# Selective attention into a hard-swish MLP: mask by selection from the fifth pair, one normalization for two heads over two banks, and moved queue work

## The chip, the cores and the metric

The kernel runs on one core of one Trainium2 chip. The metric is the device time of one execution in microseconds (us). TensorE (PE) does the matrix products, VectorE (DVE) and ScalarE (ACT) the elementwise work, GpSimd (POOL) casts, selects and issues DMAs, SyncE (SP) only issues DMAs.

## The reference

There are 8 batches of 8 heads with 576 positions and 64 channels. The attention has a decay that comes from `s`, and its output goes through a two-layer MLP.

```python
scores = scale * np.matmul(q, k.transpose(0, 1, 3, 2))        # scale = 1/8
causal = np.triu(np.ones((S, S), dtype=bool), k=1)
cum = np.cumsum(np.maximum(s, 0.0), axis=-1)
bias = -(cum[:, :, :, None] - cum[:, :, None, :])
scores = np.where(causal, -1e9, scores + np.minimum(bias, 0.0))
attn = np.exp(scores - np.max(scores, axis=-1, keepdims=True))
attn = attn / (np.sum(attn, axis=-1, keepdims=True) + 1e-09)
x = np.matmul(attn, v)      # then heads side by side: [4608, 512]
h = x @ w_in                # [512, 2048]
g = h * np.clip(h + 3.0, 0.0, 6.0) / 6.0
out = g @ w_out             # [2048, 512]
```

## The kernel before

**Attention.** The 64 heads go in 32 pairs; pair `p` holds heads 2p and 2p+1 (called head 0 and head 1 of the pair, `hh` in the code), and pairs are numbered from 0. Scores are computed transposed, keys on partitions, queries in columns. Queries and keys of a pair lie in `qks[p % 4]`, channels in rows 0 to 63, and in rows 64 to 67 the running sums of `s`, so that the decay comes out of the same product. Per head there are three score groups of 512 columns: `scores(p, hh, 0)` holds the four diagonal blocks of 128 keys, groups 1 and 2 what lies beside them. `corner(p)` does the last 64 positions of both heads. ACT takes the exponential of each into `P` (three buffers) or `PC`.

**The causal mask.** In pairs 0 to 7 (`NPROD` = 8) the diagonal group begins with one product of 512 columns that adds a large negative number above the diagonal (L377), and the corner with one of 128 columns (L441). In pairs 8 to 31 there is no such product: rows 68 to 127 of `qks` hold a stair of 60 steps that makes the excluded scores small, and after the exponential GpSimd sets them to zero with an affine select (`shut_out`, L426). The stair is copied into `qks` by GpSimd (in the iterations of pairs 5 to 7) and ACT (8 and 9) with `set_stair`.

**The order of queries.** A pair's queries and keys are loaded as tokens (`load_qk`), transposed on PE (`transpose_in`, L266 and L253) into PSUM and copied into `qks` by DVE and ACT (`transpose_out`, L310, L298, L332). In pairs 3 to 6 the queries stand in another, "mixed" order, for which these copies have runs of 16 elements (L298). The rows of running sums must then be in that order too (`load_aug`; the mixed copy of the rows is made at L840), and x is put back by the matrix `perm`.

**Values and normalization.** `av(p, hh, 0)` and `av(p, hh, 1)` multiply P with the values into a tile O of five blocks of 65 columns, the 65th being the sum of weights. `norm(p, hh)` on DVE is a reciprocal of the five sums (L503) and a product (L504) into `x`. In pairs 0 to 6, 11 and 31 `transpose_x` turns x into `xT` over PE and DVE (L518, L523), in the others `crossbar_x` does it with a DMA.

**The MLP.** It goes in blocks of 512 rows. A group `m1` is four products of 512 columns with `w_in` (L547) into `ph`; ACT makes `tr` of it (L562), DVE `gT` (L563). A group `m2` is four products with `w_out` (L574); four of them fill one `po` of 128 rows, which DVE scales and SP stores (L590, L593). `m2` takes two 128-row blocks in turn: its even steps go to one, its odd steps to the other.

**The order.** The schedule is written by hand. `group()` puts the next `m1` or `m2` where the loop over pairs calls it, by a written plan for the first blocks and then in turn. Pair 4 is the first with MLP groups; before it only attention runs. In each pair `av(p, 0, ...)` and `norm(p, 0)` stand in its own iteration, `av(p, 1, ...)` and `norm(p, 1)` in the next one. A pair from 5 on ends so:

```python
av(p, 0, 1)
norm(p, 0)
group()
```

Engines run their instructions in the order of the program, and a semaphore holds each until its inputs are ready and its output is free.

**PSUM.** There are eight banks: two for `ph`, two for `s` (scores; while `early` is set, the `ph` banks take scores too), two for `po`, one for `o`, one for `t`. O lies in `o`, or for head 1 in `po` (pairs 0 to 6) and `t` (from pair 9); transposed inputs and x lie in `t`, and before the first `m2` also in `po` (`t_bank`).

**The queues.** GpSimd issues tokens, weights (`load_w_in`, `load_w_out`) and most rows of running sums; SP issues v, the first rows, the crossbar transpositions and the outputs. `pool_mid` and `pool_end` hold GpSimd's work of a pair: select, cast of v, select. In pairs 4 to 7 `pool_mid` stood ahead of the pair's first scores in the program, without selects.

Of the kernel before, what the change touches and what calls it, by code (L numbers as in the profile page):

```python
# [18 lines left out]
def kernel(  # L19
# [31 lines left out]
    VW = 66  # L51
    NROW = 1
    NWARM = (11, 2, 6)
    HALVES = (slice(0, 288), slice(288, SEQ))
# [3 lines left out]

    grp = (np.arange(128) * 61 // 128)[None, :]
    steps_r = np.arange(1, 61)[:, None]  # L60
    stair = np.zeros((128, 2, 128), np.float32)
    stair[68:, 0] = np.where(grp < steps_r, 1.0, 0.0)
    stair[68:, 1] = np.where(grp == steps_r, NEG_BIG, 0.0)
    stair_dram = nc.inline_tensor(stair.astype(np.float16), name="stair")

# [28 lines left out]
    ident2 = keep("ident2", [128, 128], F16)  # L94
    stair_sb = keep("stair_sb", [128, 2, 128], F16)
    bias3 = keep("bias3", [128, 1], F32)
# [62 lines left out]
    def load_aug(p, eng):  # L159
        for hh in range(2):  # L160
# [6 lines left out]
            )  # L167

    def load_w_in(c):
        nc.gpsimd.dma_start(  # L170
            out=w_in_sb[:, :, 512 * c : 512 * (c + 1)],
            in_=moe_w_in[:, 512 * c : 512 * (c + 1)].rearrange(
                "(kc p) f -> p kc f", p=128
            ),
        )
# [34 lines left out]
    early = [True]  # L210
    turn = [0]

    def s_bank(shape, name):
# [4 lines left out]
    def t_bank(other, name):  # L218
        if not done[2] and other:
            return psum.tile([128, 640], F16, tag="po", bufs=2, name=name)  # L220
        return psum.tile([128, 640], F16, tag="t", name=name)
# [51 lines left out]
    def mixed(p, i):  # L273
        return i == 0 and PPB - 1 <= p < NPROD - 1

# [93 lines left out]
    def scores(p, hh, g):  # L369
        qT, kT = qk_of(p, hh)  # L370
        pt = Pof(p, hh)
        S = s_bank([128, 512], "S")
        by_product = p < NPROD
        if g == 0:
            rows = slice(0, 68 if by_product else 128)
            if by_product:
# [46 lines left out]

    def shut_out(ap, w):
        part = ap.rearrange("p (t c) -> p t c", c=w)
        nc.gpsimd.affine_select(  # L426
            out=part,
            in_=part,
            pattern=[[0, part.shape[1]], [1, w]],
            compare_op=ALU.is_ge,  # L430
            fill=0.0,
            base=0,
            channel_multiplier=-1,
        )

    def corner(p):
        S = s_bank([128, 2, 64], "Sc")
        by_product = p < NPROD
        rows = slice(0, 68 if by_product else 128)
        if by_product:  # L440
# [29 lines left out]
    def av(p, hh, part):  # L470
        va, pt = vas[p % NVA], Pof(p, hh)
        if part == 0:

            tag = "o" if not hh or NPROD - 1 <= p < NPE - 2 else "po" if p < NPROD else "t"
            O[p, hh] = psum.tile(
                [128, 5, 65], F32, tag=tag, bufs=2 if tag == "po" else 1, name="O"
            )
        o = O[p, hh]
# [11 lines left out]
        else:  # L490
# [5 lines left out]
            block(4, 4, PCs[p % 2][:, c : c + 128], start=False, stop=True)  # L496

    def norm(p, hh):
        o = O.pop((p, hh))
        if hh == 0:  # L500
# [12 lines left out]
    def transpose_x(p):  # L513
        b, hp = p // PPB, p % PPB
        x = X.pop(p)
        pt = t_bank(True, "ptx")
        for t in range(5):
# [49 lines left out]
    def m2(n, i):  # L567
        t4, fq = 2 * (i // 8) + i % 2, i % 8 // 2
        if fq == 0:
            po = psum.tile([128, 512], F32, tag="po", bufs=2, name="po")  # L570
            pos[n, t4] = po
# [120 lines left out]

    def set_stair(i, copy, heads=(0, 1)):
        for hh in heads:
            copy(
                out=qks[i][64:128, hh, :, 64 * hh : 64 * hh + 640].rearrange(
                    "p i (t c) -> p i t c", c=128
                ),
                in_=stair_sb[64:128, :, None, :].to_broadcast([64, 2, 5, 128]),
            )  # L700

    fill(nc.vector, xT[:, 0, 0:SEQ], 0.0)

    def warm(n):
        W = psum.tile([128, 512], F32, tag="o", name="W")
        for _ in range(n):
            nc.tensor.matmul(
                W, lhsT=xT[:, 0, 0:128], rhs=xT[:, 0, 0:512], start=True, stop=True
            )
# [119 lines left out]
    warm(NWARM[2])  # L829
    load_aug(1, nc.gpsimd)  # L830
    load_v(1, nc.sync)
    load_aug(2, nc.sync)
    cast_v(0)
    for i in range(2):
        load_qk(3, i)
    load_v(2, nc.sync)
    cast_v(1)
    for i in range(2):
        load_qk(4, i)
    nc.gpsimd.tensor_copy(  # L840
        out=mix(rows_of[0][0:32, 0, 0:SEQ]), in_=unmix(C["c"][0:32])
    )

# [3 lines left out]
    for p in range(NP):  # L847
# [27 lines left out]
        def pool_mid():  # L875
            if p >= NPROD:
                shut_out(Pof(p, 0)[:, 0:512], 128)
            if nxt:
                cast_v(p + 1)
            if p in (5, 6, 7):  # L880
                set_stair((p + 3) % NQK, nc.gpsimd.tensor_copy)
            if p == 13:
                new_rest()
                cum4(1, nc.gpsimd, whole)
                cum5(1, nc.gpsimd.tensor_copy, whole)

        def pool_end():
            if p >= NPROD:
                shut_out(PCs[p % 2][:, 0:128], 64)
                shut_out(Pof(p, 1)[:, 0:512], 128)  # L890
            if p >= NPROD and p != 9 and p + 2 < NP:
                if p == 14:
                    cum6(1, nc.gpsimd, whole)
                load_aug(p + 2, nc.gpsimd)

        if p >= PPB:
            for fn, c in {
                4: ((I, 2),),
                5: ((I, 3),),
                6: ((U, 0), (U, 1), (U, 2), (U, 3)),  # L900
                7: ((U, 4), (U, 5), (U, 6), (U, 7)),
            }.get(p, ()):
                fn(c)
        if PPB <= p < NPROD:
            pool_mid()
            if p == 4:
                load_aug(7, nc.gpsimd)
            elif p in (6, 7):
                load_aug(p + 2, nc.gpsimd)
# [6 lines left out]
        if p == 2:  # L916
            nc.sync.dma_start(out=stair_sb, in_=stair_dram.ap())
        if p == 10:
# [12 lines left out]
        if p < PPB:  # L931
            scores(p, 0, 0)
            scores(p, 0, 1)
            get(0)
            scores(p, 0, 2)
            corner(p)
            if p:
                av(p - 1, 1, 0)
                av(p - 1, 1, 1)
                norm(p - 1, 1)  # L940
            get(1)
            scores(p, 1, 0)
            scores(p, 1, 1)
            av(p, 0, 0)
            scores(p, 1, 2)
            if p:
                transpose_x(p - 1)
            av(p, 0, 1)
            norm(p, 0)
            continue  # L950

        if p == PPB:
            early[0] = False
            scores(p, 0, 0)
            av(p - 1, 1, 0)
            av(p - 1, 1, 1)
# [11 lines left out]
        else:  # L968
            scores(p, 0, 0)
            if p >= NPROD:  # L970
                pool_mid()
            get(0)
            group()
            scores(p, 0, 1)
# [10 lines left out]
        corner(p)  # L985
        if p in (8, 9):
            set_stair(3, nc.scalar.copy, (p - 8,))
        elif p == 11:
            new_sum()
# [7 lines left out]
        scores(p, 1, 0)  # L997
        if p >= NPROD:
            pool_end()
        if PPB < p < NPE - 1:  # L1000
# [64 lines left out]
```

## Time and profile before

| | |
|---|---|
| runs | 354.62, 355.29 and 932.81 us, median 355.29 |
| profiled execution | 354.79 us, span 353.1 us, TensorE clock 1.00 |
| PE busy | 345.1 us, 2926 matmuls |
| DVE, ACT, POOL busy | 230.2, 224.7, 169.7 us |
| second MLP matrix, L574 | 145.9 us in 576 products, 379 ns each |
| first MLP matrix, L547 | 148.1 us in 576 products, 379 ns each |
| O, L481 | 47.9 us in 896 products, 193 ns each |
| exponentials, L422 | 111.3 us in 192 |
| normalization, L503 and L504 | 64 each, 186 and 492 ns |
| select, L426, 512 columns | 48, 651 ns |
| mask product, L377 and L441 | 16 and 8, 379 and 219 ns |
| stair copies, L695 | 6 on GpSimd, 2 on ACT, 1253 and 1255 ns |

The span is the time from the first to the last instruction that the profile shows. A line "L504 DVE TENSOR_TENSOR x<-O,rl 128x320" is line 504 of the program, its engine and operation, its output and inputs, and its shape. In a group's line there follow busy time, mean duration of one, and the idle time of the engine ahead of it with what ended it. In a timeline the columns are start and length in us; matmuls are pipelined, so that a length holds the pipeline too and what one costs is read from start to start.

### The profile page before, as it was taken

The page shows a single profiled execution, that of the slowest core. Times are in us where ns is not written, and L with a number is a line of the kernel's source. Part 1 is how long each engine was busy: PE and PEld are TensorE (multiplying, and loading weights), DVE is VectorE, ACT ScalarE, POOL GpSimd, SP SyncE. Part 2 cuts the span into 40 slices and gives each one's busy share as a digit, 9 for nine tenths or more (in the row PEclk, how much of TensorE's full clock was granted, in tenths as well). Part 3 has the DMA queues.
Part 4 walks back from the last instruction along what each step waited for, and adds up shares of the span by engine and source line. Part 5 has one row for each costly group of instructions (what it writes and reads, how often), then busy time and mean ns, then how long its engine had stood idle before and what let it go on. Part 6 is the DMA issues. An engine that isn't in the chain of part 4 may idle for free.

```text
span 353.1 us, 7778 instructions
## 1 busy us (share of the span) xinstructions
PE 345.1 (98%) x2926; PEld 191.0 (54%) x2926; DVE 230.2 (65%) x476; ACT 224.7 (64%) x397; POOL 169.7 (48%) x296
## 2 busy tenths in 40 slices
PE   8999999999999999999999999999999999999995
PEld 3775666555555555555555555555555444444442
DVE  7996997676868677666666666757654544544531
ACT  6987896787787667666776666666664334443310
POOL 8977799676778656455555555555310000000000
PEclk9999999999999999999999999999999999999999
DMA  9999999999999999998798959997120100101112
GB/s 164 152 208 209 199 185 182 117 181 196 154 136 100 190 219 188 173 211 186 168 167 198 179 144 197 181 180 164 38 75 14 59 29 34 59 2 59 59 50 72
DMA packets 144782, 48.35 MB, mean 137 GB/s; under 512 B 130648, under 2 KB 139784, under 8 KB 144744
## 3 DMA queue, kind: packets, MB, share of 16 engines
q1 hardware_dynamic: 117112, 37.54, 54.0%
q0 software_dynamic: 27392, 10.03, 24.8%
q8 instruction: 23, 0.38, 0.4%
q10 hardware_dynamic: 240, 0.28, 0.2%
q14 instruction: 15, 0.12, 0.1%
HBM read 37.36 MB, written 9.44 MB: 133 GB/s over the span
## 4 chain that ended last, share of the span: by engine, by line
PE 90%; DVE 4%; ACT 3%; issue 1%; DMA 1%; ACTq 0%
PE po L574 35%; PE ph L547 34%; PE O L481 7%; PE S L403 7%; PE S L388 4%; DVE qk L310 1%; PE pt L266 1%; ACT P L422 1%; DMA s_all<-in_s_dram 1%; DVE x L504 1%; PE ptx L518 1%; PE Sc L454 1%; ACT tr L562 1%; PE S L377 1%; DVE qk L332 1%
## 5 line engine op out<-in xcount | busy, mean ns | idle before, releaser
L563 DVE SCALAR_TENSOR_TENSOR gT<-tr,ph 128x512 f16<-128x512 f32 x144 | 98.9, 687 | 97.6 <-ACT tr L562 96.5
L547 PE MATMUL ph<-xT,w_in_sb 128*128 128x512 f16 x576 | 148.1, 379 | 0.0
L574 PE MATMUL po<-w_out_sb,gT 128*128 128x512 f16 x576 | 145.9, 379 | 0.0
L562 ACT ACTIVATE tr<-ph,bias 128x512 f32<-128x512 f32 x144 | 99.0, 688 | 73.0 <-PE ph L547 70.6
L422 ACT ACTIVATE P<-S 128x512 f16<-128x512 f32 x192 | 111.3, 595 | 37.5 <-PE S L388 22.3
L547 PEld LDWEIGHTS <-w_in_sb 128*128 128x128 f16 x576 | 51.4, 97 | 44.2
L574 PEld LDWEIGHTS <-gT 128*128 128x128 f16 x576 | 50.0, 97 | 46.5 <-issue 0.2
L426 POOL TENSOR_SCALAR_AFFINE_SELECT P<-P 128x512 f16<-128x512 f16 x48 | 31.3, 651 | 44.4 <-ACT P L422 44.4
L403 PE MATMUL S<-qk 68*128 68x448 f16 (+3 forms) x256 | 49.0, 272 | 0.5 <-ACT P L422 0.5
L481 PE MATMUL O<-va,P 128*128 128x65 f16 x896 | 47.9, 193 | 0.3 <-ACT P L422 0.3
L481 PEld LDWEIGHTS <-P 128*128 128x128 f16 x896 | 39.2, 97 | 14.0 <-ACT P L422 0.5
L230 DVE COPY qk<-jt 64x768 f16<-64x768 f16 x84 | 36.8, 439 | 1.2
L403 PEld LDWEIGHTS <-qk 68*128 68x128 f16 x256 | 23.7, 98 | 24.5 <-issue 0.9
L162 POOL DMA_DIRECT2D qk<-rows_of x56 | 32.8, 588 | 1.1 <-PE S L403 0.3
L504 DVE TENSOR_TENSOR x<-O,rl 128x320 f16<-128x320 f32 x64 | 31.5, 492 | 2.2
L590 DVE TENSOR_SCALAR ob<-po 128x512 f32<-128x512 f32 (+1 forms) x36 | 24.3, 676 | 8.3 <-PE po L574 7.6
L388 PEld LDWEIGHTS <-qk 128*128 128x128 f16 (+1 forms) x256 | 18.9, 97 | 14.0 <-DVE qk L310 1.7
L426 POOL TENSOR_SCALAR_AFFINE_SELECT PC<-PC 128x128 f16<-128x128 f16 x24 | 7.0, 293 | 39.9 <-ACT PC L462 39.8
L388 PE MATMUL S<-qk 128*128 128x128 f16 (+1 forms) x256 | 24.8, 219 | 1.0 <-DVE qk L332 0.5
L206 POOL CAST va<-vraw 128x512 f16<-128x512 f32 x32 | 21.0, 656 | 4.7 <-DMA vraw<-in_v_dram 2.4
L310 DVE COPY qk<-pt 64x576 f16<-64x576 f16 x22 | 17.6, 805 | 6.2 <-ACT qk L310 5.9
L202 POOL CAST tok<-raw 128x576 f16<-128x576 f32 x28 | 18.0, 679 | 0.0
(79 smaller groups left out, 201.9 us busy)
## 6 DMA issues: line engine op xcount, KB each, us to landing
out_dram<-ob SPq DMA_DIRECT2D x35, 256.0 KB, 2.0
vraw<-in_v_dram SPq DMA_DIRECT2D x64, 128.0 KB, 4.0
raw<-in_q_dram SPq DMA_DIRECT2D x14, 288.0 KB
raw<-in_k_dram SPq DMA_DIRECT2D x14, 288.0 KB
tok<-in_q_dram POOLq DMA_DIRECT2D x18, 144.0 KB, 5.2
tok<-in_k_dram POOLq DMA_DIRECT2D x18, 144.0 KB, 5.9
w_in_sb<-in_moe_w_in_dram POOLq DMA_DIRECT2D x4, 512.0 KB, 8.5
w_out_sb<-in_moe_w_out_dram POOLq DMA_DIRECT2D x8, 256.0 KB, 7.1
```

What stands on the lines that cost most here:

```text
L162: eng.dma_start(out=qks[p % NQK][64:68, hh, :, 64 * hh : 64 * hh + SEQ], in_=rows_of[g // 32].rearrange("(r g) i t -> g r i t", g=32)[g % ...
L230: copies[par](out=qk[0:64, :, i, 128 * par : 128 * par + 256 * n].rearrange("p h (s two c) -> p h s two c", two=2, c=128)[:, :, :, 0, :], ...
L388: mm(S[:, c], lhsT=kT[rows, c], rhs=qT[rows, c], start=(j == 0 and not by_product), stop=(j == 3 and p >= NROW),)
L403: mm(S[:, c : c + w], lhsT=kT[0:68, 128 * j : 128 * (j + 1)], rhs=qT[0:68, 128 * (j + 1) : SEQ], start=(c == 0), stop=(c != 0 and p >= NROW),)
L422: nc.scalar.activation(out=pt[:, c], in_=S, func=AF.Exp, scale=0.125)
L426: nc.gpsimd.affine_select(out=part, in_=part, pattern=[[0, part.shape[1]], [1, w]], compare_op=ALU.is_ge, fill=0.0, base=0, channel_multip ...
L481: mm(o[:, i, :], lhsT=lhsT, rhs=va[:, hh, j, 0:65], **kw)
L504: nc.vector.tensor_tensor(out=X[p][:, :, hh, :], in0=o[:, :, 0:64], in1=rl.to_broadcast([128, 5, 64]), op=ALU.mult,)
L547: mm(ph, lhsT=w_in_sb[:, kc, ft * 128 : (ft + 1) * 128], rhs=xT[:, kc, n * 512 : (n + 1) * 512], start=(kc == 0), stop=(kc == NKC - 1),)
L562: nc.scalar.activation(out=tr, in_=ph, func=AF.Relu, bias=bias3[:, 0:1])
L563: nc.vector.scalar_tensor_tensor(out=gTs[n][:, ft, :], in0=tr, scalar=6.0, in1=ph, op0=ALU.min, op1=ALU.mult)
L574: mm(po, lhsT=gTs[n][:, ft, t4 * 128 : (t4 + 1) * 128], rhs=w_out_sb[:, ft, :], start=(ft == 0), stop=(ft == NFT - 1),)
```

## The change

1. **Select from the fifth pair.** The mask products stay in pairs 0 to 3 alone (`NMASK` = 4). Pairs 4 to 7 take the stair and the select. The select gets a pattern for the mixed order.
2. **A shorter stair by DMA.** The stair has seven steps of 16 columns in rows 68 to 74, in two versions, for plain and mixed order, and is loaded straight into `qks` by SP (`load_stair`); the copies on GpSimd and ACT are gone.
3. **One normalization.** A tile `OO` of two banks replaces `o` and one bank of `po`. In pairs 0 to 2 and 4 to 6 head 0's O lies in half 0 and head 1's in half 1, and one reciprocal and one product serve both (`norm_pair`), in the place of head 1's. In pairs 0 to 2 `av(p, 0, ...)` moves into the next iteration. From pair 7 on half 0 takes O, and half 1 every second 128-row block of `m2`. The transposed x uses the bank `t`, except that of pair 3.
4. **Third pair's queries mixed.** `mixed` begins with pair 2.
5. **Queues.** `pool_mid` and `pool_end` hold the selects of pairs 4 to 7 and the weight loads, behind the first scores; rows of pairs 1, 7, 8 and 9 are issued by SP; the mixed copy of the rows comes before the second cast of v. In pairs 6 to 9 the next pair's queries are copied out around a group.

```diff
+    NMASK = PPB
+    NSTAIR = 7
...
+    grp = (np.arange(128) // 16)[None, :]
+    steps_r = np.arange(1, NSTAIR + 1)[:, None]
...
+    def load_stair(p, eng):
+        eng.dma_start(
+            out=qks[p % NQK][68 : 68 + NSTAIR], in_=stair_drams[mixed(p, 0)].ap()
+        )
...
+    OO = psum.tile([128, 2, 512], F32, tag="oo", name="OO")
+
+    def paired(p):
+        return p < PPB - 1 or PPB <= p < NPROD - 1
...
     def mixed(p, i):
-        return i == 0 and PPB - 1 <= p < NPROD - 1
+        return i == 0 and PPB - 2 <= p < NPROD - 1
...
-        by_product = p < NPROD
+        by_product = p < NMASK
         if g == 0:
-            rows = slice(0, 68 if by_product else 128)
+            rows = slice(0, 68 if by_product else 68 + NSTAIR)
...
-            tag = "o" if not hh or NPROD - 1 <= p < NPE - 2 else "po" if p < NPROD else "t"
-            O[p, hh] = psum.tile(
-                [128, 5, 65], F32, tag=tag, bufs=2 if tag == "po" else 1, name="O"
-            )
+            if hh and p >= NPE - 2:
+                O[p, hh] = psum.tile([128, 5, 65], F32, tag="t", name="O")
+            else:
+                half = hh if p < NPROD - 1 else 0
+                O[p, hh] = OO[:, half, 0:325].rearrange("p (i c) -> p i c", c=65)
...
+    def norm_pair(p):
+        o = OO[:, :, 0:325].rearrange("p h (i c) -> p h i c", c=65)
+        X[p] = work.tile([128, 5, 2, D], F16, tag="x", name="x")
+        rl = work.tile([128, 2, 5, 1], F32, tag="rl2", name="rl2")
+        nc.vector.reciprocal(out=rl, in_=o[:, :, :, 64:65])
+        nc.vector.tensor_tensor(
+            out=X[p].rearrange("p i h d -> p h i d"),
+            in0=o[:, :, :, 0:64],
+            in1=rl.to_broadcast([128, 2, 5, 64]),
+            op=ALU.mult,
+        )
+
     def norm(p, hh):
+        if paired(p):
+            if hh:
+                norm_pair(p)
+            return
...
-        pt = t_bank(True, "ptx")
+        pt = t_bank(p == PPB - 1, "ptx")
...
         if fq == 0:
-            po = psum.tile([128, 512], F32, tag="po", bufs=2, name="po")
+            if len(pos) % 2:
+                po = OO[:, 1]
+            else:
+                po = psum.tile([128, 512], F32, tag="po", name="po")
...
         def pool_mid():
-            if p >= NPROD:
-                shut_out(Pof(p, 0)[:, 0:512], 128)
+            shut_out(p, Pof(p, 0)[:, 0:512], 128)
             if nxt:
                 cast_v(p + 1)
-            if p in (5, 6, 7):
-                set_stair((p + 3) % NQK, nc.gpsimd.tensor_copy)
+            for fn, c in {
+                4: ((I, 2),),
+                5: ((I, 3), (U, 0), (U, 1)),
+                6: ((U, 2), (U, 3), (U, 4)),
+                7: ((U, 5), (U, 6), (U, 7)),
+            }.get(p, ()):
+                fn(c)
...
         if p == 2:
-            nc.sync.dma_start(out=stair_sb, in_=stair_dram.ap())
+            for i in range(PPB + 1, NPROD):
+                load_stair(i, nc.sync)
+        if p in (4, 6, 7):
+            n = 7 if p == 4 else p + 2
+            if p != 4:
+                load_stair(n, nc.sync)
+            load_aug(n, nc.sync)
+        elif p == 8:
+            load_stair(10, nc.sync)
...
             get(0)
+            if p:
+                av(p - 1, 0, 0)
+                av(p - 1, 0, 1)
             scores(p, 0, 2)
             corner(p)
+            get(1)
             if p:
                 av(p - 1, 1, 0)
                 av(p - 1, 1, 1)
                 norm(p - 1, 1)
-            get(1)
             scores(p, 1, 0)
             scores(p, 1, 1)
-            av(p, 0, 0)
             scores(p, 1, 2)
             if p:
                 transpose_x(p - 1)
-            av(p, 0, 1)
-            norm(p, 0)
+            if p == PPB - 1:
+                av(p, 0, 0)
+                av(p, 0, 1)
+                norm(p, 0)
             continue
```

## The prediction

> **What bounds the kernel now.** Pairs are numbered from 0, so the fifth pair is pair 4. I read the page first: busy time, then the chain that ended last.
>
> ```profile
> PE 345.1 (98%) x2926; PEld 191.0 (54%) x2926; DVE 230.2 (65%) x476; ACT 224.7 (64%) x397; POOL 169.7 (48%) x296
> ...
> PE 90%; DVE 4%; ACT 3%; issue 1%; DMA 1%; ACTq 0%
> ```
>
> The program is TensorE from end to end. An average over stages hides where that is so, so next the windows (columns: length, then busy us of PE, PEld, DVE, ACT, POOL):
>
> ```profile
> 9.90:26.20 16.30, 15.43 (x265) 12.31 (x263) 15.04 (x32) 14.98 (x32) 14.23 (x25) 1.00 1.13 184
> ...
> 33.00:61.00 28.00, 28.00 (x318) 17.94 (x317) 23.79 (x46) 23.16 (x45) 24.18 (x33) 1.00 1.18 191
> 120.00:265.00 145.00, 145.00 (x1273) 81.36 (x1271) 96.11 (x203) 99.41 (x177) 73.61 (x137) 1.00 0.86 166
> ```
>
> Pairs 0 to 3 (9.9 to 26.2) load PE, DVE and ACT alike. From 33 on PE never idles, so there a removed column is gained and a new wait is paid in full. The timeline shows what paces pairs 0 to 3, here the step from pair 2 to pair 3:
>
> ```profile
> 20.29 0.30 ACT L462 ACTIVATE PC<-Sc 128x128 f16<-128x128 f32 x1
> 20.44 0.81 ACT L310 COPY qk<-pt 64x576 f16<-64x576 f16 x1
> ...
> 21.29 0.81 DVE L310 COPY qk<-pt 64x576 f16<-64x576 f16 x1 [0.31 <-ACT qk L310]
> ...
> 22.15 0.23 PEld L388 LDWEIGHTS <-qk 68*128 68x128 f16 x4 [0.35 <-DVE qk L310]
> 22.16 0.40 PE L388 MATMUL S<-qk 68*128 68x128 f16 x4
> ```
>
> This is a ring: first scores of pair 2 at 18.34, its three exponentials, the corner's, ACT's half of pair 3's key copy, DVE's half, first scores of pair 3 at 22.16: 3.82 us a turn.
>
> Last, the end of a pair in the steady part, around the normalization of its first head:
>
> ```profile
> 156.04 1.03 PE L547 MATMUL ph<-xT,w_in_sb 128*128 128x512 f16 x4
> 156.91 0.44 PE L481 MATMUL O<-va,P 128*128 128x65 f16 x9
> 157.11 0.69 ACT L562 ACTIVATE tr<-ph,bias 128x512 f32<-128x512 f32 x1 [0.27 <-PE ph L547]
> 157.19 0.19 PE L481 MATMUL O<-va,PC 128*128 128x65 f16 x1
> 157.22 1.03 PE L574 MATMUL po<-w_out_sb,gT 128*128 128x512 f16 x4
> 157.83 0.69 DVE L563 SCALAR_TENSOR_TENSOR gT<-tr,ph 128x512 f16<-128x512 f32 x1 [1.64 <-ACT tr L562]
> 158.44 0.19 DVE L503 RECIPROCAL rl<-O 128x5 f32<-128x5 f32 x1
> 158.66 0.49 DVE L504 TENSOR_TENSOR x<-O,rl 128x320 f16<-128x320 f32 x1
> ```
>
> PE goes from the last product into O (157.19) to the second MLP matrix (157.22) in 0.03 us. DVE, in order, first does gT of the group before (it needs ACT, which needs PE's group of 156.04) and has normalized O only at 159.15. Nobody waits for that today.
>
> **What the Trainium skill says.** "TensorE: Matmul & The Clock Gate", step-by-step section: only weight loads are pulled ahead, matmuls stay in program order, so a matmul that waits holds all behind it. The trace agrees: PE's order above is the program's. "PSUM — Partial Sum Buffer", the section on bank collisions: guard by bank; its summary says to read one bank while a matmul writes a different one. The trace agrees: L574 at 157.22 fills one bank while L504 reads another. So the chip needs no wait between the halves of OO; whether there is one is the program's affair. "VectorE: DVE Perf Modes", why PSUM operands drop a tier: fp32 from PSUM runs at single rate; L504 takes 492 ns for 320 elements. "TensorE: Matmul & The Clock Gate", HAM oscillation: idle gaps over some 3.4 us lower the clock; PEclk is 1.00 throughout here, so no run shows it.
>
> **The change part by part.** In the built program of the changed kernel I followed each wait to the instruction that satisfies it.
>
> ```profile
> L504 DVE TENSOR_TENSOR x<-O,rl 128x320 f16<-128x320 f32 x64 | 31.5, 492 | 2.2
> L426 POOL TENSOR_SCALAR_AFFINE_SELECT P<-P 128x512 f16<-128x512 f16 x48 | 31.3, 651 | 44.4 <-ACT P L422 44.4
> ...
> L377 PE MATMUL S<-shut,ident 128*128 128x512 f16 x16 | 6.1, 379 | 0.0
> ...
> L441 PE MATMUL Sc<-shut,ident 128*128 128x128 f16 x8 | 1.8, 219 | 0.0
> ```
>
> (1) Masks of pairs 4 to 7. Eight L377 and four L441 go. The 379 and 219 ns contain the pipeline; from start to start (34.17 to 34.38, 37.50 to 37.55) they cost 0.21 and 0.05 us, 0.48 a pair. Pairs 5 to 7 gain 1.45. Pair 4 gains 0.1, its ACT and DVE chain ends later. Stair rows add contraction rows, no columns.
>
> (2) GpSimd gains eight L426 (0.65) and four small ones (0.29), 6.4 us, and loses six stair copies of 1.25 and eight row issues of 0.59, 12.2. It is ahead: results are due some 5 us after the exponential. A select over the mixed order is not in the trace; between 0.65 and the 1.24 of the copy through that order (L840), I take 0.9; hidden either way. ACT loses two stair copies of 1.26, the second before PE's 0.21 wait at 71.39: gain 0.2.
>
> (3) DMA issues. Rows of pairs 1, 7, 8, 9 move from GpSimd to SP, seven stair loads of 21 KB are added there, rows of pair 2 go behind the mixed copy and the second v load. SP mostly sits in waits. The w_in part 2 is issued behind a select and a cast, about 31 instead of 28.35; it took 9.6 us, is used after 41.95 and, by step 5, 5 us later still: 0, with 2 us at most if the queue is slow. The lanes GpSimd reuses (an issue waits for the eighth before it) were free with 0.7 us of waiting in all.
>
> (4) Third pair's queries mixed: two copies of 0.45 (L298) for two of 0.80 (L310), 0.7 us of DVE, but ahead of ACT's key copy, so off the new ring below.
>
> (5) One normalization. Per pair it saves 0.35 us of DVE: one reciprocal (0.22) and one fixed part (0.13); 640 elements over two banks are not in the trace: no less than 0.7, no more than the 0.98 of two; I take 0.49 + 320 x 1.0 ns = 0.81 (1.0 ns is L590's 683 less L504's 492 over 192 elements). But it stands behind the key copies on DVE, and on PE the transposition of x, which waits for it, stands ahead of the next pair's first scores. The ring grows by 0.22 + 0.81, the transposition 0.25, the mask product now behind it 0.21, and 0.2 because 15 more products (0.47) precede the third scores: 3.8 to about 5.5 us. By that: pair 2 starts 0.8 late (its step was slower before), pair 3 1.7 more, pair 4 2.0 more (its predecessor's 15 products precede it too). Next, pair 3's second head, in half 1, waits for the normalization of half 0: 0.5 more until the first MLP group. Sum +5.0, between 0, if the order were harmless, and 7. In pairs 5 to 7 the x transposition shares a bank with the next queries: they wait 0.1 to 0.3 for L523; +0.3.
>
> (6) Two banks in one tile. From pair 7 on, half 0 takes O, half 1 every second 128-row block of the second MLP matrix. The followed waits show that each write to one half waits for the last earlier read of either half. Behind the first head's last product stands, in pairs 7, 10, 12, 14 and 18 to 31, a group into half 1, with nothing between. It waits for L504. Above: 159.15 plus 0.05 for the semaphore, less 157.22: 1.98 us. Nothing shortens it, since group, tr, gT, reciprocal and product follow from one another. The same reading at each of the 18 ends in this trace gives 1.98 every time: 35.6. Second heads of pairs 7 and 8 also lie in half 0: 60.61 + 0.05 - 59.51 = 1.15, and 0.17. Pair 8's first: 0.25. Pair 8's second O waits for DVE's copy out of half 1, which stands behind one key copy: about 1.2. Elsewhere 1 to 4 us of PE work lie between: 0.3. Together 38.7, between 35 and 42. All stands behind these on PE, which has no slack.
>
> Sum: -1.55 - 0.2 + 5.0 + 0.3 + 38.7 = +42.25. The profiled execution took 354.79 (span 353.1, 1.7 around it): 397.0. Against the median 355.29, 0.5 above it: 397.5.
>
> **The rivals.**
> - Half the stall: DVE reaches the normalization at once, a wait is then the 0.93 from 157.19 + 0.19 to the end of a 0.7 us pair of instructions. For: DVE is at 66%. Against: gT stands before it in order. 18 x 0.93 + 3: 355.3 + 3.6 + 19.7 = 378.6.
> - Only the longer ring: halves don't hold each other up on the chip. Against: the waits are in the program. 355.3 + 3.6 = 358.9.
> - Not slower: the change does what it says. PE is the bound, 12 products go (1.55), ACT's copies give 0.2, and DVE's relief closes the waits of pairs 2 to 4 (PE's 0.22 at 18.34, ACT's 1.00 before 18.84): -1.2. 352.3. It decides if x is normalized within the 1.3 us that PE spends on scores after the products, and the halves are free. For: DVE has less work. Against: key copies stand ahead.
> - Clock: 2 us gaps each 11 us let it fall. If each of the 18 were followed by 3 us at half rate: 18 x 1.5 = 27 more, 424.5. Against: gaps under 3.4.
>
> **How the numbers follow.** The forecast 0.87; half the stall 0.04; ring only 0.03; not slower 0.02; clock 0.04. Its range: low 355.3 - 1.75 + 0 + 35 = 389; high 355.3 - 1.2 + 7 + 0.6 + 42 + 2 for late weights = 405. The others lie outside with 0.13. 2% is about what a measurement of this kernel can tell from no change. Faster by more 0.01 (352.3 is within 2%), within 2% 0.05, slower 0.94.
>
> **What would show it.** Right: waits of PE for DVE at L504's successor, near 2 us each, some 40 us in all, and PE at about 87% of the span; first scores of pairs 2, 3, 4 near 19.3, 24.8, 30.8. The ring is wrong if pair 4 starts before 27. The forecast is wrong if in the steady part PE shows no idle ahead of the second matrix; half right if the waits are near 1 us.

## The result, and the profile after

The changed kernel takes 401.11 us (median of 4 runs, 400.49 to 402.86), the kernel before on the same chip 355.03. The ratio is 1.131, 95% interval 1.126 to 1.136: slower by 46 us, inside the range that was given, 3.6 above the forecast. One of the four runs of the kernel before took 932.81 us, and the ratio leaves it out. The profiled execution took 400.49, with a span of 398.7 where before had 353.1.

Line numbers are now those of the changed kernel: L585 and L615 are the two MLP matrices, L503 the products into O, L541 and L542 the normalization of one head, L525 the product of the one for two heads, L556 the transposition of x, L393 the mask product, L404 and L419 the scores. In `rest` and the runs made from it some of them are a few lines lower.

The page of the changed kernel, its busy time, its chain that ended last, and the two groups of the second MLP matrix (last columns: idle time before them, and who ended it):

```profile
PE 349.4 (88%) x2914; PEld 193.3 (48%) x2914; DVE 226.7 (57%) x464; ACT 222.1 (56%) x395; POOL 163.6 (41%) x294
...
PE 76%; DVE 12%; ACT 7%; issue 4%; ACTq 0%
...
L615 PE MATMUL OO<-w_out_sb,gT 128*128 128x512 f16 x288 | 73.8, 378 | 33.6 <-DVE x L542 33.6
...
L615 PE MATMUL po<-w_out_sb,gT 128*128 128x512 f16 x288 | 73.9, 379 | 0.0
```

PE has 12 products less to do and now stands idle for an eighth of the span. The same instruction, with the same 288 products, waits 33.6 us where it writes half 1 of OO and not at all where it writes po. The chain shows it too: from PE 90%, DVE 4%, ACT 3% to 76, 12 and 7.

The windows, by the same stretches as before:

```profile
9.90:26.20 16.30, 12.42 (x186) 9.46 (x185) 10.36 (x19) 11.76 (x25) 11.47 (x21) 0.94 1.13 173
33.00:61.00 28.00, 25.81 (x299) 16.71 (x299) 22.15 (x38) 22.87 (x45) 22.05 (x37) 1.00 1.05 174
120.00:265.00 145.00, 126.80 (x1103) 70.90 (x1101) 83.88 (x182) 86.39 (x154) 69.06 (x127) 1.00 0.78 154
```

In the 145 us of the steady part PE was busy all the time before; now 18.2 us are idle, and every other engine is less busy too: nothing became a bound, all wait. In the first stretch the granted clock (third number from the end) is 0.94 and no longer 1.00.

The end of a pair in the steady part, the same place as was shown of before (timeline):

```profile
175.76 1.03 PE L585 MATMUL ph<-xT,w_in_sb 128*128 128x512 f16 x4
...
176.91 0.19 PE L503 MATMUL OO<-va,PC 128*128 128x65 f16 x1
...
177.55 0.69 DVE L601 SCALAR_TENSOR_TENSOR gT<-tr,ph 128x512 f16<-128x512 f32 x1 [1.63 <-ACT tr L600]
...
178.15 0.19 DVE L541 RECIPROCAL rl<-OO 128x5 f32<-128x5 f32 x1
178.38 0.49 DVE L542 TENSOR_TENSOR x<-OO,rl 128x320 f16<-128x320 f32 x1
...
178.92 0.81 PE L615 MATMUL OO<-w_out_sb,gT 128*128 128x512 f16 x3 [1.82 <-DVE x L542]
```

The order on DVE is that of before: gT, reciprocal, product. What is new is that PE stands still until the product has read half 0, though it is to write half 1. From the last product into O to the second matrix it is 2.01 us; before it was 0.03: 1.98 lost. (The bracket says 1.82, as it counts from the modelled end of the last product.)

The ring of pairs 0 to 3 (timeline, first scores of pairs 2, 3 and 4, and what PE waits for ahead of them):

```profile
18.71 0.45 PE L556 MATMUL ptx<-ident,x 128*128 128x128 f16 x5 [1.93 <-DVE x L525]
19.00 0.38 PE L393 MATMUL S<-shut,ident 128*128 128x512 f16 x1
...
24.35 0.71 PE L556 MATMUL ptx<-ident,x 128*128 128x128 f16 x5 [1.83 <-DVE x L525]
24.86 0.63 PE L393 MATMUL S<-shut,ident 128*128 128x512 f16 x1
...
31.58 0.45 PE L556 MATMUL ptx<-perm,x 128*128 128x128 f16 x5 [1.99 <-DVE x L525]
...
32.33 0.39 PE L404 MATMUL S<-qk 75*128 75x128 f16 x4
```

The transposition of x waits for the one normalization (L525) and holds up the next pair's scores in each turn. From 24.86 on the same 512 columns take 0.63 us and not 0.38: the clock is at about half.

### The profile page after: what moved, and what is told of

It reads as the page before. It is cut to its first block, busy times and chain, and to the rows that moved or that the text cites. A ratio compares the mean times of both kernels' runs of the same rounds, so it can differ in the third digit from the quotient of the medians.

```text
span 398.7 us, 7762 instructions
## 1 busy us (share of the span) xinstructions
PE 349.4 (88%) x2914; PEld 193.3 (48%) x2914; DVE 226.7 (57%) x464; ACT 222.1 (56%) x395; POOL 163.6 (41%) x294
## 4 chain that ended last, share of the span: by engine, by line
PE 76%; DVE 12%; ACT 7%; issue 4%; ACTq 0%
PE ph L585 29%; PE OO L615 16%; PE po L615 15%; PE S L419 6%; ACT tr L600 4%; PE S L404 3%; DVE x L542 3%; PE O L503 3%; PE OO L503 2%; DVE qk L326 2%; DVE gT L601 2%; ACT P L438 1%; DVE rl L541 1%; DVE x L525 1%; PE ptx L556 1%
## 5 line engine op out<-in xcount | busy, mean ns | idle before, releaser
L585 PE MATMUL ph<-xT,w_in_sb 128*128 128x512 f16 x576 | 148.1, 378 | 0.1
L615 PE MATMUL OO<-w_out_sb,gT 128*128 128x512 f16 x288 | 73.8, 378 | 33.6 <-DVE x L542 33.6
L615 PEld LDWEIGHTS <-gT 128*128 128x128 f16 x576 | 51.3, 97 | 81.9 <-issue 35.6
L615 PE MATMUL po<-w_out_sb,gT 128*128 128x512 f16 x288 | 73.9, 379 | 0.0
L585 PEld LDWEIGHTS <-w_in_sb 128*128 128x128 f16 x576 | 51.3, 97 | 44.3 <-issue 0.2
L448 POOL TENSOR_SCALAR_AFFINE_SELECT P<-P 128x512 f16<-128x512 f16 x56 | 37.0, 661 | 86.7 <-ACT P L438 86.6
L419 PE MATMUL S<-qk 68*128 68x448 f16 (+3 forms) x256 | 48.8, 273 | 0.5 <-ACT P L438 0.5
L503 PEld LDWEIGHTS <-P 128*128 128x128 f16 x896 | 39.5, 98 | 15.7 <-issue 2.1
L419 PEld LDWEIGHTS <-qk 68*128 68x128 f16 x256 | 23.8, 99 | 24.7 <-issue 0.6
L246 DVE COPY qk<-jt 64x768 f16<-64x768 f16 x84 | 34.3, 409 | 1.2
L503 PE MATMUL OO<-va,P 128*128 128x65 f16 x574 | 30.2, 194 | 2.0 <-DVE ob L631 1.0
L169 POOL DMA_DIRECT2D qk<-rows_of x48 | 28.5, 597 | 0.3 <-POOL rows_of L806 0.3
L404 PE MATMUL S<-qk 75*128 75x128 f16 (+1 forms) x256 | 25.1, 220 | 0.2
L404 PEld LDWEIGHTS <-qk 75*128 75x128 f16 (+1 forms) x256 | 19.1, 98 | 12.2 <-DVE qk L348 0.6
L326 DVE COPY qk<-pt 64x576 f16<-64x576 f16 x20 | 15.9, 802 | 8.1 <-ACT qk L326 6.3
L503 PE MATMUL O<-va,P 128*128 128x65 f16 x322 | 17.3, 193 | 0.0
```

The source lines that it names most:

```text
L169: eng.dma_start(out=qks[p % NQK][64:68, hh, :, 64 * hh : 64 * hh + SEQ], in_=rows_of[g // 32].rearrange("(r g) i t -> g r i t", g=32)[g % ...
L246: copies[par](out=qk[0:64, :, i, 128 * par : 128 * par + 256 * n].rearrange("p h (s two c) -> p h s two c", two=2, c=128)[:, :, :, 0, :], ...
L326: copies[par](out=bass.AP(to.tensor, to.offset, [list(to.ap[0]), [2 * SPAD + 64, 2], [6, 96], [2, 3]],), in_=pt[64 * par : 64 * par + 64, ...
L404: mm(S[:, c], lhsT=kT[rows, c], rhs=qT[rows, c], start=(j == 0 and not by_product), stop=(j == 3 and p >= NROW),)
L419: mm(S[:, c : c + w], lhsT=kT[0:68, 128 * j : 128 * (j + 1)], rhs=qT[0:68, 128 * (j + 1) : SEQ], start=(c == 0), stop=(c != 0 and p >= NROW),)
L448: nc.gpsimd.affine_select(out=part, in_=part, pattern=pattern, compare_op=ALU.is_ge, fill=0.0, base=0, channel_multiplier=-1,)
```

## The experiments

Two questions: is it the shared tile that costs the time in the steady part, and what makes the first 35 us longer? Each edit is to the changed kernel unless said otherwise.

**Two tiles (split).** The theory: waits across the halves. The rivals: bank contention, or a late VectorE.

```diff
-    OO = psum.tile([128, 2, 512], F32, tag="oo", name="OO")
+    OO = [psum.tile([128, 512], F32, tag=f"o{h}", name=f"OO{h}") for h in range(2)]
...
-        nc.vector.reciprocal(out=rl, in_=o[:, :, :, 64:65])
+        for hh in range(2):
+            o = O.pop((p, hh))
+            nc.vector.reciprocal(out=rl, in_=o[:, :, 64:65])
```

> The changed kernel with OO as two tiles of one bank each; the two heads of a paired pair are then normalized by two reciprocals and two products back to back, at the place of the one. All else as changed, the longer ring too. Theory (waits across the halves of one tile): all 19 waits of the second matrix for L542 go, 38.7 us less, and 0.6 with pair 3's second head; two normalizations for one cost 0.35 us of VectorE in each of three turns, 1.0 more. 400.5 - 39.3 + 1.0 = 362. Rival (bank contention or a VectorE that is late anyway, tile or not): the waits before the second matrix stay, over 390. Rival (half of the stall): about 381.

Measured 365.06 us (ratio to before 1.028, 1.026 to 1.031). The group, on the page's form, and the end of the same pair (timeline):

```profile
L616 PE MATMUL OO<-w_out_sb,gT 128*128 128x512 f16 x288 | 73.9, 379 | 0.0
```

```profile
167.74 0.19 PE L503 MATMUL OO<-va,PC 128*128 128x65 f16 x1
167.77 1.03 PE L616 MATMUL OO<-w_out_sb,gT 128*128 128x512 f16 x4
...
169.21 0.49 DVE L543 TENSOR_TENSOR x<-OO,rl 128x320 f16<-128x320 f32 x1
```

The products go into the same kind of bank, right behind the last product of O, while the normalization of the other bank comes 1.4 us later: 33.6 us of waits became 0.0. Contention and a late VectorE are out. Behind pair 7's first head nothing more is lost: split is 10.59 us later than the kernel before at its last product, and 10.69 at that of the last head. The profiled execution (365.49) lies 3.5 us above the expected 362. Some 1.6 of that arise in the first 45 us, where the clock falls three times and not once (0.50 and 0.66 from 20 to 24, 0.69 and 0.50 from 26 to 30, 0.50 and 0.75 from 34 to 38), 0.5 in pairs 5 to 7; and from pair 7 on the waits were worth 37.5 and not 38.7.

**Parity (swap).** One comparison, the tile stays shared.

```diff
-            if len(pos) % 2:
+            if len(pos) % 2 == (n < 2):
                 po = OO[:, 1]
```

> The changed kernel with one comparison changed: from the third block of rows on, the even 128-row blocks of the second matrix go to half 1 of OO and the odd ones to po. The group right behind a first head's last product then writes po, and the next write into OO has 2.3 us of other products ahead. Theory: the 14 stalls of pairs 18 to 31 (27.7 us) go, though the tile is still shared; one new stall of about 2 us at the switch, and in seven pairs the first product into half 0 waits about 0.5 us for VectorE's copy out of half 1. 400.5 - 27.7 + 2 + 3.5 = 378 (373 to 383). Rival (the normalization itself, or the bank, costs PE the time): the 2 us stay in those 14 pairs, about 400.

Measured 376.19 us (1.060, 1.059 to 1.062). PE's waits for L542, the answer on waits:

```profile
PE OO L615 <- DVE x L542: 9.9, 6, 1.8
```

In the traces, against the changed kernel, the time from one first head's last product to the next is shorter by 1.98 us in each of pairs 18 to 31, 27.7 in all, and longer by 1.98 once, at the switch. The seven small waits that I had added did not come; the rest is a start 1.7 us later, with half clock in the first ring turn. So nothing about the normalization or the bank costs the time, only which product stands right behind it.

**The old order in pairs 0 to 3 (oldring).** The loop is that of before (its lines are in the diff of the change), `paired` leaves out pairs 0 to 2.

> The changed kernel with the order of before in pairs 0 to 3: products of the first head within the pair, x normalized ahead of the copies of the next keys, one normalization per head in pairs 0 to 2. The shared tile stays. Theory: the 6.9 us by which the first MLP group came late go, less the 0.6 that pair 3's second head waits across the halves, plus 0.2 for the mask product that is gone anyway: 400.5 - 6.6 = 393.9. Rival (the lateness comes from transfers or GpSimd's new order): first scores of pairs 2 to 4 stay at 19, 25, 32, time 400.

Measured 397.33 us (1.120, 1.119 to 1.122): the profiled execution gains 3.2 us, half of the 6.6 that were expected. In its trace PE waits 2.3 us at 24.07, before pair 3's first scores, for a transfer of the decay rows, and the clock is at 0.60 and 0.54 in the two stretches behind it. In the changed kernel these rows are not waited for: its ring gets to pair 3 only at 25.

**Everything but the shared tile and the ring (rest).** PSUM tiles, normalizations and loop order of before; select, stair by DMA, mixed third pair and queues as changed.

> The changed kernel with the PSUM banks, the normalizations and the order of pairs 0 to 3 of before: what is left of the change is the mask by select from pair 4 on, pair 3's queries mixed, stair rows loaded, and the new order on GpSimd and SyncE. Theory: 12 mask products (1.55 us) and a wait of 0.2 behind ACT's stair copies go, PE is the bound: 355.0 - 1.75 = 353.3. Rival (GpSimd's selects or late weights show up once the stalls don't hide them): 356 to 360.

Measured 357.30 us (1.008, 1.005 to 1.011), not faster. The first scores of pairs 2 and 3 (timeline) and the windows behind (PEclk is the third number from the end):

```profile
17.84 0.40 PE L403 MATMUL S<-qk 68*128 68x128 f16 x4
...
24.47 0.59 PE L403 MATMUL S<-qk 68*128 68x128 f16 x4 [2.86 <-DMA qk<-rows_of]
```

```profile
26.00:28.00 2.00, 2.00 (x27) 1.81 (x26) 1.41 (x4) 1.06 (x4) 1.90 (x3) 0.50 1.06 130
28.00:30.00 2.00, 2.00 (x17) 1.51 (x16) 1.47 (x3) 1.52 (x4) 0.67 (x2) 0.50 1.30 187
```

The wait for rows and the half clock after it cost more than the select brings.

**x transposed later (xlate).**

```diff
                 norm(p - 1, 1)
+            if p in (2, 3):
+                transpose_x(p - 2)
             scores(p, 1, 0)
...
-            if p:
+            if p == PPB - 1:
                 transpose_x(p - 1)
```

> The changed kernel with the transposition of x of pairs 0 and 1 moved on TensorE: from ahead of the next pair's first scores to behind the next pair's products of the second head, one pair later. Nothing else is moved. Theory (the transposition, which waits for the pair's one normalization, holds up the next first scores, which wait only for the key copy at 17.54): pairs 2 and 3 start about 1.3 us earlier each, at 17.6 and 22.3, pair 4 keeps its own wait of 2 us and starts at about 29, and with the gaps the drop of the clock after 24.35 (1.4 us) goes: 400.5 - 4 = 396.5. Rival (VectorE's chain or the transfers set the turn): the first scores come less than 0.5 us earlier, 400.

Measured 399.77 us (1.126, 1.124 to 1.128). In the timeline:

```profile
17.78 0.40 PE L404 MATMUL S<-qk 68*128 68x128 f16 x4 [0.60 <-DVE qk L326]
...
23.55 0.38 PE L404 MATMUL S<-qk 68*128 68x128 f16 x4 [1.58 <-DMA qk<-rows_of]
```

Pair 2 starts at 17.78, as worked out (17.6): it was the transposition that held it to 19.21. Pair 3 would follow, but now waits for its rows, pair 4 starts at 29.89 and not 32.33, and then PE runs at half clock from about 30.5 to 37 and gives nearly all of it back. In this execution, the slowest of its four, it falls once more, to 0.50 behind the stall of 1.82 us at pair 7's first head (68 to 71), which costs 1.55 us. The cause was right, the gain of 4 us was not to be had.

**Gaps filled (filler, filler3).** Products without use in PE's gaps ahead of the transposition; filler3 fills the third gap too.

```diff
+            if p in (1, 2):
+                W = s_bank([128, 512], "W")
+                for _ in range(7):
+                    mm(
+                        W.rearrange("p (t c) -> p t c", c=128),
+                        lhsT=ident2,
+                        rhs=shut[:, None, :].to_broadcast([128, 4, 128]),
+                        start=True,
+                        stop=True,
+                    )
             if p:
                 transpose_x(p - 1)
```

> The changed kernel with seven products without use (512 columns each, 1.5 us together, into a bank of their own) ahead of the transpositions of x of pairs 0 and 1, where TensorE idles 1.9 us. No work is taken away. If idle gaps lower the clock: PEclk stays at 1.00 from 24 to 28 where it was 0.53 and 0.62, the products after 24.35 take 0.38 for 512 columns instead of 0.63, and the time falls by 1.4 us to 399. If the clock fell for another reason, it falls again, and the time stays at 400.5 or rises.

> The changed kernel with products without use ahead of the transpositions of x of pairs 0, 1 and 2 (seven, seven and eight of 512 columns): the gap before 31.58 is filled too, which was left in the run with two fills, where the clock fell after it instead. If idle gaps lower the clock: PEclk 1.00 in every stretch from 18 to 42, first MLP group at about 32.9 without a slow stretch after it, and 400.5 - 1.4 - (what fell after 32 in some runs) = 398.8. If not, a stretch at about half clock shows again somewhere between 18 and 42, and the time is as with two fills, 400.

Measured 399.96 (1.127, 1.125 to 1.130) and 399.87 us (1.129, 1.126 to 1.133). Windows of the changed kernel, then of filler:

```profile
24.00:26.00 2.00, 1.65 (x11) 1.24 (x12) 0.75 (x2) 0.00 (x0) 2.00 (x4) 0.53 0.84 139
26.00:28.00 2.00, 2.00 (x33) 1.88 (x32) 0.91 (x2) 1.12 (x3) 2.00 (x4) 0.62 1.17 157
32.00:34.00 2.00, 1.41 (x37) 1.17 (x34) 1.18 (x4) 0.60 (x1) 0.52 (x1) 1.00 1.23 197
```

```profile
24.00:26.00 2.00, 1.69 (x27) 1.25 (x26) 0.95 (x2) 0.46 (x1) 2.00 (x4) 1.00 1.03 153
26.00:28.00 2.00, 2.00 (x48) 1.75 (x45) 1.01 (x3) 1.75 (x5) 1.95 (x4) 1.00 1.29 174
32.00:34.00 2.00, 1.92 (x18) 1.23 (x18) 0.71 (x3) 0.18 (x1) 1.68 (x3) 0.53 1.27 211
```

In these profiled executions the clock stayed full where the gaps were filled, and fell behind the one that was left. With all three filled it is 1.00 from 18 to 42. But of filler3's four runs two took 399.15 us with a mean clock of 0.999, the others 400.58 and 402.52 with 0.994 and 0.991: something still lowered it there, at a place that no trace shows. So it fits that idle time lowers the clock, at 1.2 to 1.4 us a time here, but filling these gaps doesn't prevent it, and one traced execution of each kernel doesn't prove that the gaps are the whole cause.

**Pair 2's queries in the old order (unmix), and the masks back (mask8).** Both are edits of rest.

```diff
-        return i == 0 and PPB - 2 <= p < NPROD - 1
+        return i == 0 and PPB - 1 <= p < NPROD - 1
...
     load_aug(1, nc.sync)
+    load_aug(2, nc.sync)
```

> As the run with the banks, normalizations and order of before (rest), but pair 2's queries in the old order, so that its rows no longer wait for the mixed copy and are loaded right behind pair 1's, ahead of the third v load; the mixed copy goes back to the end of GpSimd's list. What is left of the change: mask by select from pair 4 on, stair rows loaded, GpSimd and SyncE in the new order otherwise. Theory (the 2.9 us for which pair 2's first scores waited for their rows, and the half clock after it, are what makes rest slower): both go, 353.3, faster than before by 0.5%. Rival (the rows are late because SyncE's queue is full, mixed or not): the wait stays above 1 us, 356.

> As unmix, with the masks of pairs 4 to 7 by products again and without their selects (the stair rows are loaded but pairs 4 to 7 don't use them). Theory: 12 mask products cost 1.55 us on TensorE, which is the bound: 1.5 us above unmix, about 354.8. Rival (the selects delay the products by as much as they save): within 0.4 us of unmix.

Measured: unmix 355.22 (1.0018, 1.0001 to 1.0035), mask8 355.86 us (1.0030, 1.0014 to 1.0046). These two expectations, and that of ringrows below, name the wrong pair: first scores stand at 17.84, 19.83 and 24.47 in rest, one for each head, so the late rows at 24.47 are pair 3's. Moving pair 2's rows ahead still helped in the profiled run of unmix, where nothing waits for rows; but mask8 shows a wait of 1.0 us for rows of pair 1, and unmix's runs spread from 354.3 to 359.7 where those of before lie within 354.5 to 355.9. Neither came out as expected: unmix is 1.9 us above the forecast, and mask8 is 0.64 above unmix, between the 1.5 of the theory and the 0.4 of its rival.

The trace of unmix shows what the select is worth. Against before, unmix leads by 0.22 us more with each head of pairs 5 to 7, 1.34 in all: the price of the mask products. Then:

```profile
50.75 0.38 PE L403 MATMUL S<-qk 75*128 75x128 f16 x4
...
50.87 0.80 DVE L325 COPY qk<-pt 64x576 f16<-64x576 f16 x1
...
51.73 0.41 PE L281 MATMUL pt<-ident,tok 96*128 96x96 f16 x6 [0.59 <-DVE qk L325]
```

The next pair's queries are copied out around a group, the second copy comes late, and the keys' transposition waits for the same bank. The lead falls to 0.64 and ends at 0.34.

**Copies in one piece (unsplit), more of the queue put back (best).**

```diff
-            if NPROD - 1 <= p + 1 < NPE:
-                pt = transpose_in(p + 1, 0)
-                transpose_out(p + 1, 0, pt, pars=(0,))
-                group()
-                transpose_out(p + 1, 0, pt, pars=(1,))
-            else:
-                get(0)
-                group()
+            get(0)
+            group()
```

> As unmix, but the copies of the next queries are not parted around a group in pairs 6 and later. Theory: in unmix TensorE's 12 mask products were gained (the lead over before grows by 0.22 a head to 1.34 us), and then 0.59 were given back in one wait of pair 8's key transposition for the parted copy in the same bank; without it 355.2 - 0.5 = 354.7, the same as before within 0.3%. Rival (another wait takes its place): 355.2.

> As unmix (banks, normalizations, order of pairs 0 to 3 and pair 2's queries of before; mask by select from pair 4 on), with three more steps back: pair 1's rows on GpSimd, pair 4's stair rows loaded with the others in pair 2 rather than ahead of the third v load, and the copies of the next queries not parted around a group in pairs 6 and later. What is left is the select, the loaded stair rows, and GpSimd's order in pairs 4 to 7. Theory: pair 7's wait of 0.59 us for the parted copy goes, and with SyncE's queue as before no run waits for rows: 354.8 - 1.5 = 353.3 (352.8 to 353.8), the first version faster than before. Rival (the select's gain is given back elsewhere): 354.3 or more.

Measured: unsplit 355.06 (1.0016, 1.0003 to 1.0028), best 359.23 us (1.012, 1.010 to 1.015). The 0.59 is gone from unsplit's trace, but another wait took its place, as the rival had it (answer on waits):

```profile
PE ph L567 <- DVE gT L583: 0.7, 2, 0.4
```

Both stand at the group right behind the keys' transposition, for pair 7 at 46.28 and for pair 8 at 53.42, where unmix had waited just ahead of that transposition; and pair 3's rows came 0.9 us late besides; unmix and unsplit don't differ. In best PE waits at the first scores of pair 4:

```profile
26.53 0.49 DVE L524 TENSOR_TENSOR x<-O,rl 128x320 f16<-128x320 f32 x1
...
27.85 0.38 PE L403 MATMUL S<-qk 75*128 75x128 f16 x4 [2.30 <-DVE x L524]
```

The profile names DVE, which had been done for 0.83 us. These products read nothing of L524; they are the first to read stair rows, whose load I had moved back to 20.9 us. So the stair's landing is the likely releaser, though the trace doesn't name it. A second wait follows, for the corner's select:

```profile
34.72 0.61 POOL L218 CAST va<-vraw 128x512 f16<-128x512 f32 x1 [4.28 <-DMA vraw<-in_v_dram]
...
37.05 0.20 PE L501 MATMUL O<-va,PC 128*128 128x65 f16 x1 [1.12 <-POOL PC L447]
```

GpSimd stood until 34.72 for v, whose cast is ahead of that select in its order: the select is hidden only as long as the v loads are on time. The stair load is a new need of the select, and the place the change gave it, ahead of the third v load, was not free to change. No version tried beats the kernel before.

**Old ring with pair 2's rows early (ringrows).**

> As oldring (the changed kernel with the order of pairs 0 to 3 of before, the shared tile kept), with pair 2's queries in the old order and its rows loaded right behind pair 1's. Theory: oldring's 397.3 held 2.3 us of waiting for these rows and about 1.2 of low clock after it, which the longer ring hides in the changed kernel; both go: 393.8. That is the 6.6 us of the longer ring alone. Rival (the ring is worth only the 3.2 us that oldring gained): 397.

Measured 396.66 us (1.118, 1.115 to 1.120): the rival's number. PE again waits 2.1 us for pair 3's rows, at 24.52, and the clock falls to 0.75 and 0.50 behind it. Pair 3's rows are issued on SyncE at 16.0 in before and in unmix, in time for first scores at 22.2, and at 16.4, 16.8 and 16.8 in rest, oldring and ringrows, where they are waited for until 24.1 to 24.5. But in xlate they are issued at 16.0 and waited for until 23.5, and in unsplit at 17.8 and only until 23.3. So the time of issue doesn't decide: from issue to landing it takes longer in some kernels than in others, at a time when all queues are loaded, and it was only just in time before. Which of the added transfers is in its way was not settled.

## Why the prediction was right, and where its sum was off

Its main term stands. Along the profiled execution, at the same instructions of both traces:

| stretch | predicted | measured |
|---|---|---|
| to the first MLP group | +5.0 (ring, and pair 3's second head) | +6.94 (33.77 for 26.83) |
| from there to the end of pair 7's first head | -1.25 (masks -1.55, bank +0.3) | +1.11 |
| from there to the end | +38.5 (halves 38.7, ACT's copies -0.2) | +37.55 |
| sum | +42.25 | +45.6 |

The forecast came near because the last stretch, which could be read from the trace of before wait by wait, makes up most of the sum. The first two were forecast at 3.75 us together and came to 8.05; that they are small against the rest is what kept the total in its range.

- **Two banks in one tile (6).** The 18 stalls of 1.98 us came one by one, in the pairs named. Pair 7's second head gave 0.97 (worked out 1.15) and pair 8's second O 0.72 (about 1.2). Of the 0.25 and 0.17 of pair 8's two normalizations nothing came; instead the first O of pair 11, at 103.43, waited 0.60 for VectorE's copy out of half 1, where all the other places together were put at 0.3. Split and swap show the mechanism. The advice of the Trainium skill to guard by bank ("PSUM — Partial Sum Buffer", bank collisions), which the prediction quoted, agrees with split: PE writes one bank at 167.77 and VectorE reads the other at 169.21, and nothing waits.
- **The ring (5).** First scores, counted as in the prediction from the first product with queries: 19.21, 25.28 and 32.33 where 19.3, 24.8 and 30.8 were predicted; the product over two banks takes 0.82 (0.81). The term that was too small is that of pair 4: from 24.35 to 27.46 PE did the work that took 1.72 from 18.71 to 20.43, in 3.11 us. These 1.39 are the clock, and 0.43 of them are already in pair 3's 25.28; in filler, where the clock stays full there, pair 4's first scores stand at 31.10. Two of the other runs of the changed kernel had lower means of the clock, which fits the 0.6 us between the profiled execution and the median. I had the clock as a rival for the stalls of the steady part, where it did not fall in this execution (once in that of xlate), and not for the ring, where it did.
- **Masks (1).** The price was right, 0.22 a head in unmix, but "pairs 5 to 7 gain 1.45" was given back at once. In the changed kernel, from start to start, PE loses 0.60 and 0.48 us waiting for the x copy in the bank that x and the queries now share (0.3 was charged in all), and in the iteration of pair 7 another 0.37 for the queries' copy parted around a group and 1.03 at the transposition of x, which now has the bank of the next keys. The sum charged neither of the last two. With them the stretch, forecast as a gain of 1.25, lost 1.11. The select itself was priced right: some 0.9 us in the mixed order (0.9 taken), and in the changed kernel PE waits for none.
- **DMA issues (3).** Priced at 0, and in the changed kernel nothing shows, but "0" rested on the queue having time to spare, and what hides the late rows is the longer ring. With the ring taken away 2.1 to 2.9 us of waiting for rows appear (oldring, rest, ringrows). The rival "not slower" (352.3) would have failed on this, without the shared tile too: rest has neither the shared tile nor the longer ring, and is still 0.8% slower.

## What to carry to other kernels

A PSUM tile over two banks is one thing to the program's waits: before two users share it, ask which of them stands right behind the other's last read, and price that wait on the engine that has no slack. Swapping which user comes next can remove most of it for one comparison. And where a kernel starts with several engines and the DMA queues all full, an edit can be priced at nothing only with the cover named: when the cover went here, a late transfer and a half clock came out from under it.

## What the runs showed of the hardware that was not expected

TensorE's granted clock fell to 0.50 behind gaps of 1.5 to 2.9 us in the first 35 us, for 3 to 7 us. The length of a gap alone does not decide: 1.93 us ahead of 18.71 left it at 1.00 in the changed kernel, and 1.93 us ahead of 18.87 was followed by 0.50 in swap. Likewise 1.82 us of idle time at 18 pair ends in the steady part left it at 1.00 in the changed kernel's trace, but in that of xlate it fell behind the first of them:

```profile
66.00:68.00 2.00, 1.61 (x15) 0.96 (x15) 0.41 (x2) 0.26 (x1) 0.00 (x0) 0.95 1.77 145
68.00:70.00 2.00, 2.00 (x10) 0.84 (x9) 1.53 (x2) 0.33 (x1) 1.43 (x3) 0.50 0.41 26
```

The mean clock also goes with the spread of the changed kernel's four runs: 400.49 and 400.60 us with a mean clock of 0.996, 401.61 with 0.989, 402.86 with 0.983. The Trainium skill, "TensorE: Matmul & The Clock Gate", section "What's actually happening", says that the ratio is half or full and is judged over a free-running window of some 3.4 us. The 0.50 and the spread between runs fit that. It gives at least one idle window as what comes before the half rate; but the longest gap ahead of a fall here was 2.9 us (rest), so a whole idle window is not needed. What share of idle time is enough was not measured.
